# Attention beside a feed-forward network on one core: in the second half of the tokens, two exponentials and the gates share one stay of ScalarE's table

## The chip, the core and the metric

One NeuronCore of a Trainium2 chip runs the whole kernel. The metric is the device time of one launch in microseconds (us), taken as the median of several runs. The core has five engines that work side by side, each through its own queue in order: TensorE (PE; its weight loads are PEld), VectorE (DVE), ScalarE (ACT), GpSimd (POOL) and SyncE (SP), which here only issues transfers. An engine whose next instruction waits for a semaphore holds up everything behind it in its queue.

## The reference

There are 2048 tokens of 512 channels. Everything is fp32.

```python
g = sigmoid((x * gate_w).sum(-1, keepdims=True))           # one gate for each token
q, k, v = (x @ wqkv), split into 32 heads of 16             # scale = 16 ** -0.5
logits[s, w] = q[s] . k[s - 2 * w] * scale                  # w = 0..7, masked before the start
o[s] = sum_w softmax(logits[s])[w] * v[s - 2 * w]
a = o @ wo
b = (gelu(x @ w_gate) * (x @ w_up)) @ w_down                # 1792 hidden channels
return g * a + (1 - g) * b
```

Attention sees only tokens at an even distance, so even and odd tokens never meet. The kernel does the 1024 even tokens first and the 1024 odd ones after them. It calls the two halves parities (`par` 0 and 1).

## The kernel before

**The feed-forward network.** `ffn(par)` runs over 14 channel blocks `f` of 128 hidden channels. `gate_up` computes a block in seven products (a Strassen-like scheme, L459), each of 6 matmuls in split precision. They accumulate in PSUM banks called `p`, of which there are four in turn: `X_`, `W_`, `Z_` and one for the down products. ScalarE copies partial sums out (`W_ <- X_` L539, `copy` L464) and applies gelu (L554 and L570). VectorE adds (`add`, L469, reads a `p` bank), multiplies gelu by up (L473) and takes the low half of the split (`hl`, L476), which needs ScalarE's high half (`hh`, L475). The last product of a block, `a22` by `t4`, and its gelu L570 are put into the next block (`fourth()`). The down products (L502) read `hh` and `hl`.

**The attention.** Each parity has four units of 128 channels (8 heads), `(par, 0)` to `(par, 3)`. A unit goes through these steps, nearly all on VectorE:

- `scores`: four times a product of shifted keys and queries (L225) and a sum over 16 channels (L228), into the tile `lg`; then the mask (L232).
- `exps`: maximum over the 8 places (L241; recorded in `PEAK`), subtraction (L243; recorded in `LESS`), then the exponential on ScalarE (L245).
- `gates(par)`: sigmoid of the gate's logits: an exponential on ScalarE (`en`, L167), then three small steps on VectorE (L170 to L172) that give `g` and `gc`. Once for each parity.
- `softmax` and `gated`: sum (L257), reciprocal (L259), times the gate (L267), times `lg` (L269).
- `mix`: four times values by weights (L287), three sums (L291, L293, L295), and transposes to DRAM (L300, L302).

ScalarE holds one table of functions at a time. Gelu and exp are in different ones, so between a gelu and an exp stands an ACT_TABLE_LOAD. In the first parity the exponentials of units 0 and 1 and the gates already stand together (L245 twice, then L167).

**The order.** `attention()` is a generator that writes these steps in small portions; `pull(budget)` in the feed-forward code takes portions by a price in microseconds. A scheduler then sets each engine's order from priorities, dependencies and its own timeline. `ordered` adds a fixed order on one engine, `after` a wait across engines, and `paced` ties a step to the last matmul.

**The slots.** The tile `kq` holds in its first part the keys of a unit `(par, 0)` and later the values of a unit, in its last part the queries. In `load_kq` the last load of unit (1, 2), its queries, waits for `PEAK`, and in `mix` the value loads of unit (1, 0) do:

```python
for ins in load_slots(v, VS[par, hh][c]):
    if par and not u:
        after(ins, PEAK[-1])
```

These loads (L201, L209, L210) go through SP's queue with the feed-forward's weight loads (`g<-ws` L412, `raw` L438 and L440, `r` L392).

Of the kernel before, what the change touches and what calls it, by code (L numbers as in the profile page):

```python
# [12 lines left out]
AF = mybir.ActivationFunctionType  # L13
# [35 lines left out]
def tile_gated_mix(ctx: ExitStack, tc: tile.TileContext, xt, wqkv, wff, wo, out):  # L49
    nc = tc.nc  # L50
# [69 lines left out]
    z = pool.tile([P, 2, NP], F32, name="z")  # L120
# [42 lines left out]
        if not hh:  # L163
            nc.scalar.activation(z[:, par, jj:jj + 1], ps[:, CU:CU + 1], AF.Copy)

    def gates(par, ex=None):
        first = nc.scalar.activation(en, z[:, par], AF.Exp, scale=-1.0)  # L167
        if ex:
            ordered(first, ex)
        nc.vector.tensor_scalar_add(en, en, 1.0)  # L170
        nc.vector.reciprocal(g[:, par], en)
        nc.vector.tensor_scalar(gc[:, par], g[:, par], -1.0, 1.0, op0=OP.mult, op1=OP.add)  # L172
# [19 lines left out]
    def load_kq(par, u):  # L192
        hh, c = divmod(u, 2)
        k, q = slots_of(u > 0), KQ["a"][:, 2 * NP - 1:]
        if u == 1:
            q = pool.tile([P, 2, BT * UC], F32, name="tb").rearrange("p a (b c) -> p (a b) c", c=UC)
        LG[par, u] = k, q
        if not u:
            return
        loads = load_slots(k, KS[par, hh][c])  # L200
        loads.append(nc.sync.dma_start(q, QS[par, hh][c].rearrange("(p j) d -> p j d", j=NP)))  # L201
        if not par and u < NU - 1:
            for ins in loads:
                after(ins, SCORED[-1])
        elif (par, u) == (1, 2):
            after(loads[-1], PEAK[-1])
# [13 lines left out]
    def scores(par, u):  # L220
        k, q = LG[par, u]
        lg = pool.tile([P, UH, NP, W], F32, name="lg", bufs=2)
        for jj in range(0, NP, 2):
            prod = pool.tile([P, 2, W, UC], F32, name="prod")
            paced(nc.vector.tensor_tensor(prod, spans(k, jj), q[:, jj:jj + 2, None, :].to_broadcast([P, 2, W, UC]),  # L225
                                          op=OP.mult))
            yield 2.3
            nc.vector.tensor_reduce(two_of(lg, jj), prod.rearrange("p j w (h d) -> p (j w) h d", d=DH), axis=AX.X,  # L228
                                    op=OP.add)
            yield 2.3  # L230
        first = lg[:1, :, :NP - 1, :W - 1]
        SCORED[:] = [nc.vector.tensor_tensor(  # L232
            first, first, mask[:1, None, :NP - 1, :W - 1].to_broadcast([1, UH, NP - 1, W - 1]), op=OP.min)]
        LG[par, u] = lg

    def exps(par, *us):

        for u in us:
            lg = LG[par, u]
            m = pool.tile([P, UH, NP], F32, name="m")  # L240
            PEAK[:] = [nc.vector.tensor_reduce(m, lg, axis=AX.X, op=OP.max)]  # L241
            yield 0.7
            LESS[:] = [nc.vector.tensor_tensor(lg, lg, m[:, :, :, None].to_broadcast([P, UH, NP, W]), op=OP.subtract)]  # L243
            yield 0.7
        ex = [nc.scalar.activation(LG[par, u], LG[par, u], AF.Exp, scale=DH ** -0.5) for u in us]  # L245
        if len(us) > 1:
            after(ex[0], LESS[-1])
            ordered(ex[1], ex[0])
            ordered(ex[0], COPIED[-1])
            gates(par, ex[1])  # L250

    def softmax(par, u):
        if par or u != 1:
            yield from exps(par, u) if par or u else exps(par, u, u + 1)
        lg = LG[par, u]
        m = pool.tile([P, UH, NP], F32, name="m")
        nc.vector.tensor_reduce(m, lg, axis=AX.X, op=OP.add)  # L257
        yield 0.7
        nc.vector.reciprocal(m, m)  # L259
        LG[par, u] = lg, m  # L260

    def gated(par, u):
        lg, m = LG[par, u]
        LG[par, u] = lg
        if par and not u:
            gates(par)
        nc.vector.tensor_tensor(m, m, g[:, par, None, :].to_broadcast([P, UH, NP]), op=OP.mult)  # L267
        yield 0.4
        nc.vector.tensor_tensor(lg, lg, m[:, :, :, None].to_broadcast([P, UH, NP, W]), op=OP.mult)  # L269
        yield 0.7  # L270

    def mix(par, u, pause):
        lg = LG.pop((par, u))
        hh, c = divmod(u, 2)
        v = slots_of(u == NU - 1)
# [3 lines that stand above are left out]
            elif (par, u) == (0, NU - 1):  # L279
                after(ins, LESS[-1])  # L280
        yield pause
        tb = pool.tile([P, 2, BT * UC], F32, name="tb")
        for jj in range(0, NP, 2):
            if jj % BT == 0:
                o = pool.tile([P, 4, BT, 32], F32, name="o")
            prod = pool.tile([P, 2, W, UC], F32, name="prod")
            paced(nc.vector.tensor_tensor(prod.rearrange("p j w (h d) -> p (j w) h d", d=DH),  # L287
                                          spans(v, jj).rearrange("p j w (h d) -> p j w h d", d=DH),
                                          two_of(lg, jj)[:, :, :, None].to_broadcast([P, 2 * W, UH, DH]), op=OP.mult))
            yield 2.3  # L290
            nc.vector.tensor_tensor(prod[:, :, :4], prod[:, :, :4], prod[:, :, 4:], op=OP.add)  # L291
            yield 1.2
            nc.vector.tensor_tensor(prod[:, :, :2], prod[:, :, :2], prod[:, :, 2:4], op=OP.add)  # L293
            two = [prod[:, :, i].rearrange("p j (b c) -> p b j c", b=4) for i in range(2)]
            nc.vector.tensor_tensor(o[:, :, jj % BT:jj % BT + 2], *two, op=OP.add)  # L295
            yield 1.1

            if jj % BT == BT - 2:
                t = tb[:, jj // BT]
                nc.vector.transpose(t, o.rearrange("p b t c -> p (b t c)"))  # L300
                for a in range(4):
                    nc.sync.dma_start(OS[par, u, jj // BT][:, :, a].rearrange("b i c -> i b c"),  # L302
                                      t[32 * a:32 * a + 32].rearrange("p (b c) -> p b c", b=4))
                yield 0.7
# [3 lines left out]
    def after(ins, other, cls=mybir.DependencyClass.Sync):  # L308

        tc.add_manual_dep(ins.ins, other.ins.name, mybir.DependencyInfo(cls, mybir.DependencyReason.SCHED_ONLY),  # L310
                          reason="pace")
# [4 lines left out]
    def ordered(ins, other):  # L316
        after(ins, other, mybir.DependencyClass.NoSync)

    def need(*key):
        while key not in done:  # L320
            yield None

    def attention():
        units = [(0, u) for u in range(NU)] + [(1, u) for u in range(NU)]
        yield from need(0, 0)
        load_kq(0, 0)
        yield from scores(0, 0)
        load_kq(0, 1)
        yield from scores(0, 1)
        yield from need(0, 1)  # L330
        scored, mixed = 2, False
        for i, un in enumerate(units):
            if scored == i:
                yield from need(un[0], un[1] // 2 * 2)
                load_kq(*un)
                if un[1]:
                    yield LOAD
                else:
                    load_kq(un[0], 1)
                yield from scores(*un)  # L340
                scored += 1
                mixed = False
            yield from softmax(*un)
            if un == (1, 0):
                yield from scores(*units[scored])
                scored += 1
                yield from need(un[0], 1)
            yield from gated(*un)


            to = units[scored] if scored < len(units) else None
            ahead = to and (to[0], to[1] // 2 * 2) in done
            if ahead:
                load_kq(*to)
            yield from mix(*un, LOAD if mixed else 0.0)
            done.add((*un, "o"))
            mixed = not ahead
            if ahead:
                yield from scores(*to)
                scored += 1  # L360

    fill = attention()
    credit = [0.0]

# [114 lines left out]
    late, COPIED = [], []  # L479
# [740 lines left out]
    en = pool.tile([P, NP], F32, name="en")  # L1220
# [51 lines left out]
```

## Time and profile before

| | |
|---|---|
| median of 3 runs | 597.06 us (596.82 to 597.29) |
| the profiled execution's own time | 596.87 us |
| its span, first to last instruction | 594.8 us |
| busy: PE, DVE, ACT, POOL | 590.1, 529.4, 389.9, 89.2 us |
| granted clock of TensorE | 0.999 |
| ACT_TABLE_LOADs | 18 of 1283 ns: 7 before an exponential of logits (L245), 1 before the gates' (L167), 7 before L570, 2 before L554, 1 at the start (L787) |

All times inside the trace are from the span's start. A row of a timeline has the start, the duration, the engine, the line, the operation, output <- input, the shape and the count, and in brackets how long the engine stood idle before it and what ended that. Successive instructions of one engine overlap slightly at their ends, so the distance between starts is what one costs in a row of work. The second parity's feed-forward runs from about 315 us to the end. The work that the change touches lies between 345 and 460 us.

### The profile page before, as it was taken

Reading aid. Unit: us, or ns where it says so; the run is one execution under the profiler, and the core shown is the slowest. Engines: PE = TensorE matmul, PEld = TensorE weight load, DVE = VectorE, ACT = ScalarE, POOL = GpSimd, SP = SyncE. Lnnn points to the kernel's source line nnn. Section 1 sums busy time; section 2 is a strip of 40 time slices with the busy share of each in tenths; the row PEclk is TensorE's granted clock in tenths of the full one; section 3 lists DMA queues with packets and bytes.
Section 4 is the critical chain, followed back from the end, with each engine's and each line's share of the span. In section 5 each row is a group of like instructions: output and inputs, shape, how many; then the busy total and the mean of one; then the engine's idle time right before and its main releaser. Section 6 shows DMA issues by size and latency. Waiting matters only on the chain.

```text
span 594.8 us, 8195 instructions
## 1 busy us (share of the span) xinstructions
PE 590.1 (99%) x2778; PEld 494.1 (83%) x2778; DVE 529.4 (89%) x618; ACT 389.9 (66%) x668; POOL 89.2 (15%) x121
## 2 busy tenths in 40 slices
PE   9999999999999999999999999999999999999997
PEld 6889988888888888888889988888888888888886
DVE  5997979899998999799989888999999989799952
ACT  5845556787679767788773375677668666885532
POOL 0501001111111111102035000111111111101300
PEclk9999999999999999999999999999999999999999
DMA  8789897988989898998589948795967796737924
GB/s 316 264 250 244 238 306 217 261 245 200 273 215 300 225 261 230 240 312 304 192 249 306 276 137 264 168 244 145 272 157 226 183 269 157 220 109 193 143 57 155
DMA packets 80449, 134.18 MB, mean 226 GB/s; under 512 B 8092, under 2 KB 46362, under 8 KB 80152
## 3 DMA queue, kind: packets, MB, share of 16 engines
q1 hardware_dynamic: 62890, 97.67, 49.9%
q0 software_dynamic: 12576, 32.97, 28.4%
q10 hardware_dynamic: 4942, 3.01, 1.6%
q8 instruction: 22, 0.36, 0.3%
q14 instruction: 19, 0.16, 0.1%
HBM read 68.30 MB, written 38.86 MB: 180 GB/s over the span
## 4 chain that ended last, share of the span: by engine, by line
PE 99%; DVE 0%; ACT 0%; issue 0%
PE p L459 45%; PE acc L502 13%; PE p L502 13%; PE acc L130 8%; PE acc L787 8%; PE p L720 5%; PE p L787 5%; PE acc L720 2%; PE p L79 1%; DVE r L766 0%; ACT rt L768 0%; DVE zero L73 0%
## 5 line engine op out<-in xcount | busy, mean ns | idle before, releaser
L459 PE MATMUL p<-S,g 128*128 128x512 f32 x672 | 166.5, 389 | 0.0
L459 PEld LDWEIGHTS p<-S,g 128*128 128x128 f32 x672 | 125.7, 188 | 25.8
L459 PE MATMUL p<-A,g 128*128 128x512 f32 x504 | 126.7, 390 | 0.0
L459 PEld LDWEIGHTS p<-A,g 128*128 128x128 f32 x504 | 94.3, 188 | 19.6
L417 POOL DMA_DIRECT2D g<-raw x40 | 34.5, 862 | 280.3 <-ACT g L416 208.8
L228 DVE TENSOR_REDUCE lg<-prod 128x128 f32<-128x2048 f32 x32 | 72.9, 2279 | 0.1
L502 PE MATMUL p<-d,hh 128*128 128x512 f32 x224 | 68.5, 389 | 0.0
L502 PE MATMUL acc<-d,hh 128*128 128x512 f32 x224 | 58.1, 389 | 0.0
L287 DVE TENSOR_TENSOR prod<-kq,lg 128x2048 f32<-128x2048 f32 x24 | 54.7, 2279 | 0.9 <-PE p L459 0.5
L421 ACT ACTIVATE g<-raw 128x1024 fp32r<-128x1024 f32 (+1 forms) x40 | 39.5, 991 | 19.0 <-PE p L459 19.0
L502 PEld LDWEIGHTS acc<-d,hh 128*128 128x128 f32 x224 | 42.0, 188 | 8.7
L502 PEld LDWEIGHTS p<-d,hh 128*128 128x128 f32 x224 | 42.0, 188 | 8.7
L416 ACT ACTIVATE g<-raw 128x1024 fp32r<-128x1024 f32 (+1 forms) x40 | 39.5, 987 | 12.0 <-DVE raw L398 4.6
L469 DVE TENSOR_TENSOR c<-p,s 128x512 f32<-128x512 f32 x56 | 37.8, 682 | 6.8 <-PE p L459 6.0
L464 ACT ACTIVATE s<-p 128x512 f32<-128x512 f32 x56 | 33.2, 594 | 15.0 <-PE p L459 13.5
L476 DVE TENSOR_TENSOR hl<-c,hh 128x512 fp32r<-128x512 f32 x56 | 38.1, 680 | 5.5 <-ACT hh L475 5.5
L502 PE MATMUL p<-d,hl 128*128 128x512 f32 x112 | 42.8, 389 | 0.0
L475 ACT ACTIVATE hh<-c 128x512 fp32r<-128x512 f32 x56 | 35.1, 628 | 10.7 <-DVE c L473 10.6
L473 DVE TENSOR_TENSOR c<-c 128x512 f32<-128x512 f32 x56 | 38.2, 682 | 4.3 <-ACT c L570 4.1
L518 ACT ACTIVATE rt<-p 128x512 f32<-128x512 f32 x48 | 28.2, 595 | 20.1 <-PE p L502 20.1
L291 DVE TENSOR_TENSOR prod<-prod 128x1024 f32<-128x1024 f32 x32 | 39.0, 1218 | 0.2
L130 PE MATMUL acc<-d,A 128*128 128x256 f32 (+1 forms) x288 | 37.9, 281 | 0.0
(183 smaller groups left out, 982.0 us busy)
## 6 DMA issues: line engine op xcount, KB each, us to landing
g<-raw POOLq DMA_DIRECT2D x27, 512.0 KB, 6.6
raw<-wff SPq DMA_DIRECT2D x42, 256.0 KB, 3.7
ws<-g SPq DMA_DIRECT2D x14, 768.0 KB, 6.2
g<-ws SPq DMA_DIRECT2D x14, 768.0 KB, 5.4
r<-wff SPq DMA_DIRECT2D x28, 256.0 KB, 4.8
d<-r POOLq DMA_DIRECT2D x24, 256.0 KB, 6.4
g<-raw POOLq DMA_DIRECT2D x13, 384.0 KB, 6.4
os<-tb SPq DMA_DIRECT2D x64, 64.0 KB, 3.8
```

The costliest lines, as they stand in the source:

```text
L130: LAST[:] = [nc.tensor.matmul(ps[:, :cn], a[:, t], w[:, c0:c0 + cn], start=(kc == 0 and n == 0), stop=(kc == KC - 1 and n == 2))]
L228: nc.vector.tensor_reduce(two_of(lg, jj), prod.rearrange("p j w (h d) -> p (j w) h d", d=DH), axis=AX.X, op=OP.add)
L287: paced(nc.vector.tensor_tensor(prod.rearrange("p j w (h d) -> p (j w) h d", d=DH), spans(v, jj).rearrange("p j w (h d) -> p j w h d", d=D ...
L291: nc.vector.tensor_tensor(prod[:, :, :4], prod[:, :, :4], prod[:, :, 4:], op=OP.add)
L416: nc.scalar.activation(lo, raw, AF.Copy, scale=-1.0)
L421: ins = nc.scalar.activation(hi, raw, AF.Copy)
L459: LAST[:] = [nc.tensor.matmul(ps, w_, a_, start=(start and kc == 0 and n == 0), stop=(kc == 1 and n == 2), skip_group_check=True)]
L473: nc.vector.tensor_tensor(ge, ge, up, op=OP.mult)
L476: nc.vector.tensor_tensor(hl_, ge, hh_.bitcast(F32), op=OP.subtract)
L502: ins = nc.tensor.matmul(pp, a[:, ts], w, start=(i == 0 and n == 0 and gr == 0), stop=(i == 1 and n == 2), skip_group_check=True)
L720: ins = nc.tensor.matmul(pa, a, b, start=(first and n == 0), stop=(last and n == 2), skip_group_check=True)
L787: return lambda *args, **kw: self.add(getattr(self.eng, name)(*args, **kw))
```

## The change

Three things move, all in parity 1. The exponentials of units (1, 0) and (1, 1) are issued together by one call of `exps`, with `gates(1)` behind them. For that, the scores of (1, 1) are written ahead of the softmax of (1, 0) instead of behind it. And the tie of the first exponential to the last PSUM copy (`COPIED`) holds for parity 0 alone, as `exps` with two units now runs in parity 1 too.

```diff
-    def gates(par, ex=None):
-        first = nc.scalar.activation(en, z[:, par], AF.Exp, scale=-1.0)
-        if ex:
-            ordered(first, ex)
+    def gates(par, ex):
+        ordered(nc.scalar.activation(en, z[:, par], AF.Exp, scale=-1.0), ex)
...
             ordered(ex[1], ex[0])
-            ordered(ex[0], COPIED[-1])
+            if not par:
+                ordered(ex[0], COPIED[-1])
             gates(par, ex[1])
...
     def softmax(par, u):
-        if par or u != 1:
-            yield from exps(par, u) if par or u else exps(par, u, u + 1)
+        if u != 1:
+            yield from exps(par, u) if u else exps(par, u, u + 1)
...
         LG[par, u] = lg
-        if par and not u:
-            gates(par)
...
-            yield from softmax(*un)
             if un == (1, 0):
                 yield from scores(*units[scored])
                 scored += 1
                 yield from need(un[0], 1)
+            yield from softmax(*un)
             yield from gated(*un)
```

Lines below the edits get smaller numbers: L245 becomes L243, L241 becomes L239, L257 becomes L256, L287 becomes L284, and from L340 on each is smaller by 3 (L539 becomes L536, L570 L567, L469 L466, L473 L470, L502 L499). The text uses the numbers of before.

**ScalarE, where the gates and the first exponential stand.** Before, the gates (`en`) come while the last value projections are still copied out (`c`), with a load of the exp table and, two instructions on, one of the gelu table:

```order
L167 ACT_TABLE_LOAD
L167 ACTIVATE en_580<-z_113 128x8
L160 ACTIVATE c_3578<-acc3_3565 128x256
L464 ACTIVATE s_3589<-p_3582 128x512
L570 ACT_TABLE_LOAD
L570 ACTIVATE c_3597<-p_3213 128x512
```

The exponential of unit (1, 0), whose logits are `lg_3360`, comes one block later, again between two loads. Now both loads at the gates are gone, that exponential has moved two blocks on, and there stand, between the copy `W_ <- X_` (`p_3936`) of block 4 and the gelu of block 3 (`c_3965`), both units' logits (`lg_3360` and `lg_3622`) and the gates:

```order
L536 ACTIVATE p_3936<-p_3929 128x512
L243 ACT_TABLE_LOAD
L243 ACTIVATE lg_3360<-lg_3360 128x512
L243 ACTIVATE lg_3622<-lg_3622 128x512
L167 ACTIVATE en_580<-z_113 128x8
L567 ACT_TABLE_LOAD
L567 ACTIVATE c_3965<-p_3786 128x512
L413 ACTIVATE g1_3980<-raw_3783 128x1024
L461 ACTIVATE s_3954<-p_3947 128x512
```

The copy of `Z_` (`s_3954`) now stands behind that gelu. In the whole program 18 table loads become 14: the pair at the gates and the pair around the exponential of unit (1, 1) are gone, and one later load stands at L554 instead of L570.

**VectorE, behind that stay.** Before, in the same block 4, the adds that free the banks `Z_` (`p_3945`) and `X_` (`p_3925`) stand among the first quarters of `mix` (1, 0):

```order
L295 TENSOR_TENSOR o_3908<-prod_3909 128x4x64
L469 TENSOR_TENSOR c_4004<-p_3945,s_3976 128x512
L257 TENSOR_REDUCE m_4410<-lg_3648 128x64
L287 TENSOR_TENSOR prod_3981<-kq_268,lg_3360 128x2048
L473 TENSOR_TENSOR c_3995<-c_3995,c_4004 128x512
L259 RECIPROCAL m_4410<-m_4410 128x64
L469 TENSOR_TENSOR c_4029<-p_3925,s_3952 128x512
```

Now both units' softmax and gating and the first product of `mix` (1, 0) stand ahead of the first of these adds (`c_4007<-p_3947`). These 12 instructions begin with `c_3965`, which needs the gelu behind the stay; the add of `X_` (`c_4028`) follows three further on:

```order
L470 TENSOR_TENSOR c_3965<-c_3965,c_3887 128x512
L264 TENSOR_TENSOR m_3901<-m_3901,g_114 128x64
L170 TENSOR_SCALAR gc_579<-g_114 128x8
L266 TENSOR_TENSOR lg_3360<-lg_3360,m_3901 128x512
L256 TENSOR_REDUCE m_4410<-lg_3622 128x64
L258 RECIPROCAL m_4410<-m_4410 128x64
L284 TENSOR_TENSOR prod_3922<-kq_268,lg_3360 128x2048
L473 TENSOR_TENSOR hl_3969<-c_3965,hh_3968 128x512
L264 TENSOR_TENSOR m_4410<-m_4410,g_114 128x64
L288 TENSOR_TENSOR prod_3922<-prod_3922 128x2x512
L266 TENSOR_TENSOR lg_3622<-lg_3622,m_4410 128x512
L466 TENSOR_TENSOR c_4007<-p_3947,s_3978 128x512
```

On PE the products of block 4 are the same 66 matmuls from its first product to the first product of block 5, with `a22` by `t4` of block 3 moved one product earlier and some down products moved.

**SP, the loads for `kq`.** Before, the queries of unit (1, 2) (`qs11`) and the values of unit (1, 0) (`vs10`) stand on both sides of a weight load:

```order
L440 DMA raw_3666<-wff 128x2x256
L201 DMA kq_268<-qs11_104 128x1024
L412 DMA g0_3801<-ws40_1335 128x1536
L209 DMA kq_268<-vs10_100 128x896
L210 DMA kq_268<-vs10_100 128x1024
```

Now they stand ten places further on, behind weight loads of the following blocks and the keys of unit (1, 2), and in one piece. `PEAK` is now the maximum of unit (1, 1), since one call of `exps` takes both:

```order
L207 DMA v_862<-ks11_102 128x896
L208 DMA v_862<-ks11_102 128x1024
L435 DMA raw_3926<-ws61_1466 128x512
L437 DMA raw_3926<-wff 128x2x256
L389 DMA r_3924<-wff 128x512
L199 DMA kq_268<-qs11_104 128x1024
L207 DMA kq_268<-vs10_100 128x896
L208 DMA kq_268<-vs10_100 128x1024
L409 DMA g0_4067<-ws60_1605 128x1536
```

## The prediction

> **What bounds the kernel now.** I read the page's first part and its chain first, then the busy time by stretches, then the timelines of the engines around the edit.
>
> ```profile
> PE 590.1 (99%) x2778; PEld 494.1 (83%) x2778; DVE 529.4 (89%) x618; ACT 389.9 (66%) x668; POOL 89.2 (15%) x121
> ...
> PE 99%; DVE 0%; ACT 0%; issue 0%
> ```
>
> TensorE is busy for 590.1 of 594.8 us, and the chain that ended last is TensorE from end to end. In the stretches (columns: length, then busy time of PE, PEld, DVE, ACT, POOL, then clock, transfer share, GB/s) the two that the edit rearranges, and the tail:
>
> ```profile
> 380.00:400.00 20.00, 20.00 (x90) 16.55 (x89) 19.50 (x20) 13.64 (x23) 2.95 (x4) 1.00 0.93 234
> 400.00:420.00 20.00, 20.00 (x90) 16.55 (x89) 19.79 (x25) 14.07 (x22) 1.70 (x2) 1.00 0.68 178
> ...
> 570.00:595.00 25.00, 21.25 (x94) 17.27 (x92) 7.47 (x12) 4.55 (x8) 0.00 (x0) 0.97 0.31 106
> ```
>
> TensorE never pauses there, and the granted clock is 1.00. Only 594.8 - 590.1 = 4.7 us of the span are without a matmul, and 25.00 - 21.25 = 3.75 us of these are the last output copies and stores. So work taken off ScalarE or VectorE gives nothing back by itself: the change takes no matmul away, and there is no pause in the middle to close. It can only open one. The question is whether some bank or operand now comes later than TensorE asks for it.
>
> **The change part by part.** The table loads first (timeline of ScalarE):
>
> ```profile
> 346.86 1.28 ACT L167 ACT_TABLE_LOAD   x1
> 348.16 0.21 ACT L167 ACTIVATE en<-z 128x8 f32<-128x8 f32 x1
> ...
> 349.82 1.28 ACT L570 ACT_TABLE_LOAD   x1
> ...
> 367.65 1.28 ACT L245 ACT_TABLE_LOAD   x1
> 368.94 0.64 ACT L245 ACTIVATE lg<-lg 128x512 f32<-128x512 f32 x1
> 369.48 0.62 ACT L475 ACTIVATE hh<-c 128x512 fp32r<-128x512 f32 x1
> ...
> 375.80 0.61 ACT L539 ACTIVATE p<-p 128x512 f32<-128x512 f32 x1
> 376.43 1.28 ACT L570 ACT_TABLE_LOAD   x1
> 377.72 0.60 ACT L570 ACTIVATE c<-p 128x512 f32<-128x512 f32 x1
> ...
> 390.01 0.58 ACT L539 ACTIVATE p<-p 128x512 f32<-128x512 f32 x1 [0.76 <-PE p L459]
> ```
>
> Four of 18 loads go, 4 x 1.28 = 5.1 us of ScalarE. Worth on the span: nothing, since ScalarE is busy 66% of it and TensorE did not wait.
>
> Two waits of VectorE go as well (timeline of VectorE, idle time before the row in brackets):
>
> ```profile
> 348.40 0.17 DVE L170 TENSOR_SCALAR en<-en 128x8 f32<-128x8 f32 x1 [2.44 <-ACT en L167]
> ...
> 362.22 0.67 DVE L241 TENSOR_REDUCE m<-lg 128x64 f32<-128x512 f32 x1
> ...
> 369.61 0.69 DVE L257 TENSOR_REDUCE m<-lg 128x64 f32<-128x512 f32 x1 [2.69 <-ACT lg L245]
> ```
>
> That is 2.44 + 2.69 = 5.1 us. They don't turn into a shorter span either; until 390 us they only let VectorE run ahead of TensorE, and it then waits for the gelu outputs of blocks that TensorE has not finished.
>
> The cost is in block 4, where the stay now stands. I walk the queues from TensorE's fixed marks (timeline of TensorE; the last product of block 3 ahead of its add, the first products of blocks 4 and 5, and `a22` by `t4` of block 4):
>
> ```profile
> 385.73 1.52 PE L459 MATMUL p<-S,g 128*128 128x512 f32 x6
> ...
> 388.45 1.52 PE L459 MATMUL p<-A,g 128*128 128x512 f32 x6
> ...
> 403.41 1.52 PE L459 MATMUL p<-A,g 128*128 128x512 f32 x6
> ...
> 406.59 1.52 PE L459 MATMUL p<-A,g 128*128 128x512 f32 x6
> ```
>
> From 388.45 to 403.41 are 66 matmuls, 0.2267 us each, in both kernels.
>
> ScalarE: the copy L539 starts at 390.01. By the distances of the rows above, the load follows 0.63 later (375.80 to 376.43), at 390.64; the first exponential 1.29 later, at 391.93; the second 0.54 later (368.94 to 369.48) and the gates' another 0.54 later, at 393.01; the gelu's load 0.21 later, at 393.22; the gelu 1.29 later, from 394.51 to 395.11.
>
> Do the exponentials have to wait for VectorE? The add of block 3 that reads the product of 385.73 can start when that ends, 385.73 + 1.52 = 387.25. Behind it stand one multiply, the maximum L241 and the subtraction L243, 0.6 us each: the subtraction is done at about 389.7, 2.2 us before 391.93. So no.
>
> VectorE: its multiply L473 of that gelu starts about 0.03 behind it (348.16 + 0.21 to 348.40), at 395.15. In front of the adds that free the banks stand the instructions that the order shows. Their prices are distances between starts in this piece of before:
>
> ```profile
> 400.15 2.28 DVE L287 TENSOR_TENSOR prod<-kq,lg 128x2048 f32<-128x2048 f32 x1
> 402.35 0.69 DVE L473 TENSOR_TENSOR c<-c 128x512 f32<-128x512 f32 x1
> 402.95 0.55 DVE L259 RECIPROCAL m<-m 128x64 f32<-128x64 f32 x1
> 403.41 0.63 DVE L469 TENSOR_TENSOR c<-p,s 128x512 f32<-128x512 f32 x1
> 403.95 1.22 DVE L291 TENSOR_TENSOR prod<-prod 128x1024 f32<-128x1024 f32 x1
> 405.08 0.22 DVE L267 TENSOR_TENSOR m<-m,g 128x64 f32<-128x64 f32 x1
> 405.22 0.69 DVE L476 TENSOR_TENSOR hl<-c,hh 128x512 fp32r<-128x512 f32 x1
> 405.82 0.69 DVE L293 TENSOR_TENSOR prod<-prod 128x512 f32<-128x512 f32 x1
> 406.42 0.69 DVE L269 TENSOR_TENSOR lg<-lg,m 128x512 f32<-128x512 f32 x1
> ```
>
> L287 takes 2.20, L291 1.13, L259 0.46, L267 0.14, the 512-wide ones 0.60. So: L473 0.60, L267 0.14, L172 about 0.1, L269 0.60, L257 0.60, L259 0.46: the first product of `mix` stands at 395.15 + 2.50 = 397.65. Then L287 2.20, L476 0.60, L267 0.14, L291 1.13, L269 0.60 = 4.67: the add of `Z_` starts at 402.32 and ends 0.69 later, at 403.01. TensorE asks for that bank at 403.41: 0.4 us to spare, where before there were more than four:
>
> ```profile
> 398.48 0.67 DVE L469 TENSOR_TENSOR c<-p,s 128x512 f32<-128x512 f32 x1
> ```
>
> The add of `X_` stands three steps of 0.60 later, from 404.12 to 404.81. In the new order TensorE asks for it with `a22` by `t4` right behind the six matmuls of 403.41, at 404.77 (before: at 406.59). That is 0.04 us too late, so I put 0 to 0.3 us here for the small gaps between dependent instructions that the sum leaves out, and take 0.1.
>
> The first product of `mix` also needs the value loads, which now wait for the maximum of unit (1, 1). Before, SP had the three out 0.03 to 1.4 us behind the maximum of unit (1, 0) (timeline of SP, then the DMA issues between 355 and 380 us, then of the whole page; the last number is issue to landing):
>
> ```profile
> 362.92 0.33 SPq L201 DMA_DIRECT2D kq<-qs  x1
> ...
> 364.25 0.58 SPq L210 DMA_DIRECT2D kq<-vs  x1
> ```
>
> ```profile
> kq<-vs SPq DMA_DIRECT2D x1, 512.0 KB, 7.1
> ```
>
> ```profile
> kq<-vs SPq DMA_DIRECT2D x6, 512.0 KB, 8.2
> ```
>
> Now the maximum ends at about 389.1 (387.25 + 2 x 0.6, and 0.67 for itself). Without the weight load between them the three go out 0.42 apart (1.33 us for three steps before), the last at 390.0. It lands at 390.0 + 7.1 = 397.1, or by the page's median at 398.2, against the 397.65 at which VectorE gets there. I take 397.1, from the row of this very load: no wait, but 0.55 us from one.
>
> Behind that, VectorE lags. From 404.72, the end of the step of the add of `X_`, to the second transposes of `mix` (1, 0) stand three more rounds of L287, L291 and L293 (3.93 each), eight steps of 0.60 and four of about 0.4: 404.72 + 11.8 + 4.8 + 1.6 = 422.9, against 420.67 before, 2.2 us later. The banks and halves that TensorE asks for up to 465 us keep more than 1 us in that walk, and the orders agree again at the end. The lag is absorbed at the latest where VectorE idled before:
>
> ```profile
> 420.67 0.70 DVE L300 STREAM_TRANSPOSE tb<-o 128x512 f32<-128x512 f32 x1
> ...
> 485.98 0.69 DVE L476 TENSOR_TENSOR hl<-c,hh 128x512 fp32r<-128x512 f32 x1 [1.81 <-ACT hh L475]
> ```
>
> The sum: -5.1 us of loads and -5.1 us of waits, worth 0, and +0.1 us of pause at 404.8. On the profiled execution, 596.87 us with 594.8 of span, that makes 597.0; against the median, 597.06, which lies 0.2 higher, 597.2. A measurement of this kernel can tell about 0.2%, 1.2 us, from no change, so this is no change.
>
> **A rule against it.** ScalarE's loads are followed here at once: L539 ends at 376.41 and the load starts at 376.43, the load ends at 377.71 and the gelu starts at 377.72. The Trainium skill's page "ScalarE: Activation LUTs", section "What ACT_TABLE_LOAD costs", has 1283 ns for a load, as here, but adds a drain of about 1380 ns for each switch of set. By that page the gelu of the stay would come 2 x 1.38 = 2.76 us later than I put it.
>
> **The rivals.**
>
> *The values land late (slower, 0.13).* For it: 0.55 us of margin on a path of SP, queues and memory, and a page median that is already 0.55 us too late. Against: the one earlier pair landed in 7.1 us. Every 0.1 us past 397.65 is 0.1 us of pause at `X_`. It decides from 1.2 us late on (landing after 398.85, 8.9 us from issue); a landing in 10 to 13 us, at 400 to 403, gives 2.4 to 5.4 us: 599.6 to 602.6.
>
> *VectorE's lag opens a pause later (slower, 0.07).* If the lag of 2.2 us meets a bank that TensorE wants without any margin left, up to 2.2 us are lost there; it decides from 1.2 us on: 598.4 to 599.4. Against it: nowhere in before does TensorE wait, though VectorE is busy 19.8 of 20 us in the stretch to 420.
>
> *ScalarE is parked in the stay (slower, 0.04).* If VectorE's subtraction comes after 391.93 instead of at 389.7, gelu, copies and adds all move by the excess. It decides from 2.2 + 1.2 = 3.4 us of error in my walk; 5 us of error gives 2.8 us: 600.0.
>
> *A switch costs more than its load (slower, 0.02).* With a gap of 1.4 us at both switches, the rows shown would have to be the exception: both adds come 2.76 us later, and the pause at `X_` grows to about 2.8 us, 600.0. That is the case of the page's rule; the rows above speak against it.
>
> *It comes out faster (0.02).* It would need a shorter tail or fewer matmul cycles; 3.75 us at the end is all there is, and its order is unchanged. More than 0.3 us, 596.7, I can't find.
>
> **How the numbers follow.** Forecast: a pause of 0 to 1.1 us, chance 0.72, 597.2 us. Slower: 0.13 + 0.07 + 0.04 + 0.02 = 0.26. Faster by over 0.2%: 0.02. The range starts at 596.7, below the fastest of the runs by the noise of before, and goes to 599.4, which holds the forecast, the lag's rival and the small end of the late values: 0.72 and about 0.10 of the 0.26.
>
> **What would show it.** Right: no pause of TensorE longer than 0.3 us between 315 and 590 us; 14 table loads; no wait of VectorE at L170; L257 waiting some 2 to 3 us once, until about 392.6; the gelu at about 394.5. Wrong: a wait of VectorE's first `mix` product for `kq<-vs` around 397 us, then a pause of TensorE before the product at 403.41 or the one behind it; or ScalarE waiting for VectorE ahead of the first exponential; or a busy time of TensorE that is not 590.1 us.

## The result

The changed kernel takes 600.34 us (median of 9 runs, 599.37 to 601.45) beside 597.06 us before. The ratio is 1.005, with a 95% interval of 1.0041 to 1.006: it is slower by 0.5%, 3 us. Measured again later beside other runs of before, the ratio was 1.0042 (1.0028 to 1.0056). The profiled execution took 600.01 us with a span of 598.2 us, 3.4 us more than before.

In this part lines have the numbers of the changed kernel: L536 is the copy `W_ <- X_`, L567 the gelu of `a22` by `t4`, L466 the adds, L473 the low half `hl`, L284 the first step of `mix`, L515 the copy `rt <- p` of a down product, L499 the down products. The experiments' kernels have a few lines more, so that their numbers differ by some units. The builder is the scheduler that sets each engine's order, and a mark of TensorE is the start of a matmul that stands at the same place in both runs.

### The profile page after: what moved, and what is told of

It is laid out like the page before. It is cut to its first block, busy times and chain, and to the rows that moved or that the text cites. A ratio compares the mean times of both kernels' runs of the same rounds, so it can differ in the third digit from the quotient of the medians.

```text
span 598.2 us, 8193 instructions
## 1 busy us (share of the span) xinstructions
PE 590.8 (99%) x2778; PEld 493.5 (83%) x2778; DVE 531.4 (89%) x618; ACT 384.2 (64%) x664; POOL 89.2 (15%) x121
## 4 chain that ended last, share of the span: by engine, by line
PE 95%; DMA 2%; DVE 1%; issue 0%; ACT 0%; SPq 0%; DVEq 0%; ACTq 0%
PE p L456 43%; PE acc L499 12%; PE p L499 12%; PE acc L130 8%; PE acc L784 7%; PE p L717 5%; PE p L784 5%; PE acc L717 2%; DMA kq<-vs 1%; DMA raw<-xt 1%; DVE prod L284 0%; DVE c L466 0%; ACT g L413 0%; DVE c L470 0%; DVE lg L266 0%
## 5 line engine op out<-in xcount | busy, mean ns | idle before, releaser
L499 PE MATMUL p<-d,hh 128*128 128x512 f32 x224 | 68.4, 390 | 0.0
L499 PE MATMUL acc<-d,hh 128*128 128x512 f32 x224 | 58.6, 390 | 0.0
L284 DVE TENSOR_TENSOR prod<-kq,lg 128x2048 f32<-128x2048 f32 x24 | 54.7, 2278 | 0.9 <-PE p L456 0.5
L499 PEld LDWEIGHTS acc<-d,hh 128*128 128x128 f32 x224 | 42.0, 188 | 9.1 <-DMA d<-r 0.3
L499 PEld LDWEIGHTS p<-d,hh 128*128 128x128 f32 x224 | 42.0, 188 | 9.0 <-ACT p L493 0.3
L470 DVE TENSOR_TENSOR c<-c 128x512 f32<-128x512 f32 x56 | 38.3, 684 | 8.1 <-ACT c L567 7.8
L466 DVE TENSOR_TENSOR c<-p,s 128x512 f32<-128x512 f32 x56 | 37.9, 684 | 6.5 <-PE p L456 5.5
L473 DVE TENSOR_TENSOR hl<-c,hh 128x512 fp32r<-128x512 f32 x56 | 38.0, 681 | 5.0 <-ACT hh L472 5.0
L499 PE MATMUL p<-d,hl 128*128 128x512 f32 x112 | 42.4, 389 | 0.0
L515 ACT ACTIVATE rt<-p 128x512 f32<-128x512 f32 x48 | 27.8, 590 | 15.3 <-PE p L499 14.9
```

The lines of the kernel that those rows point to most:

```text
L470: nc.vector.tensor_tensor(ge, ge, up, op=OP.mult)
L473: nc.vector.tensor_tensor(hl_, ge, hh_.bitcast(F32), op=OP.subtract)
L499: ins = nc.tensor.matmul(pp, a[:, ts], w, start=(i == 0 and n == 0 and gr == 0), stop=(i == 1 and n == 2), skip_group_check=True)
```

## The profile after

The busy time and the chain (page of the changed kernel, its first and fourth part):

```profile
PE 590.8 (99%) x2778; PEld 493.5 (83%) x2778; DVE 531.4 (89%) x618; ACT 384.2 (64%) x664; POOL 89.2 (15%) x121
...
PE 95%; DMA 2%; DVE 1%; issue 0%; ACT 0%; SPq 0%; DVEq 0%; ACTq 0%
```

TensorE does the same 2778 matmuls in nearly the same busy time. What is new lies between them: the chain now leaves TensorE for 5% of the span. The stretches (columns as in the prediction) say where:

```profile
380.00:400.00 20.00, 20.00 (x90) 16.56 (x89) 16.22 (x22) 15.00 (x25) 2.55 (x3) 1.00 0.95 269
400.00:420.00 20.00, 19.79 (x86) 15.75 (x86) 19.86 (x25) 12.55 (x20) 1.70 (x2) 1.00 0.78 185
420.00:440.00 20.00, 18.33 (x82) 14.86 (x81) 19.54 (x18) 10.84 (x18) 2.57 (x3) 1.00 0.82 213
440.00:460.00 20.00, 20.00 (x90) 16.56 (x89) 18.54 (x21) 13.75 (x23) 1.77 (x3) 1.00 0.81 226
```

A full stretch has 90 matmuls (x90). The second has 86 and the third 82: 4 and 8 matmuls of 0.227 us are missing, 0.9 and 1.8 us, at a clock of 1.00. There are two pauses here.

**The stay itself** went as forecast (timeline of ScalarE). TensorE is 0.7 us later here than before, so 0.7 is to be added to the forecast's times:

```profile
390.78 0.58 ACT L536 ACTIVATE p<-p 128x512 f32<-128x512 f32 x1 [0.30 <-PE p L456]
391.38 1.28 ACT L243 ACT_TABLE_LOAD   x1
392.68 1.16 ACT L243 ACTIVATE lg<-lg 128x512 f32<-128x512 f32 x2
393.74 0.19 ACT L167 ACTIVATE en<-z 128x8 f32<-128x8 f32 x1
393.94 1.28 ACT L567 ACT_TABLE_LOAD   x1
395.24 0.60 ACT L567 ACTIVATE c<-p 128x512 f32<-128x512 f32 x1
```

**The first pause.** TensorE (timeline), the last down products ahead of block 5 and the twelve matmuls of its `X_` and of `a22` by `t4`:

```profile
403.67 0.61 PE L499 MATMUL p<-d,hl 128*128 128x512 f32 x2
404.35 3.44 PE L456 MATMUL p<-A,g 128*128 128x512 f32 x12
```

Two matmuls are 0.45 us, so the twelve are 404.35 - 404.12 = 0.23 us late, and they take 3.44 us where an undisturbed row of twelve takes 2.88 (below, at 434.38). Together that is 0.8 us. What they wait for are VectorE's adds (timeline of VectorE):

```profile
395.87 0.69 DVE L470 TENSOR_TENSOR c<-c 128x512 f32<-128x512 f32 x1 [1.20 <-ACT c L567]
...
396.73 0.69 DVE L266 TENSOR_TENSOR lg<-lg,m 128x512 f32<-128x512 f32 x1
397.46 0.69 DVE L256 TENSOR_REDUCE m<-lg 128x64 f32<-128x512 f32 x1
398.18 0.55 DVE L258 RECIPROCAL m<-m 128x64 f32<-128x64 f32 x1
398.93 2.29 DVE L284 TENSOR_TENSOR prod<-kq,lg 128x2048 f32<-128x2048 f32 x1 [0.19 <-DMA kq<-vs]
...
403.61 0.68 DVE L466 TENSOR_TENSOR c<-p,s 128x512 f32<-128x512 f32 x1
...
405.41 0.68 DVE L466 TENSOR_TENSOR c<-p,s 128x512 f32<-128x512 f32 x1
```

L284 starts 3.06 us behind L470, not 2.50: 0.37 us are longer steps, mainly the two around the second unit's sum L256 (0.73 and 0.72 us, where the forecast took 0.60), and 0.19 us are a wait for the values. The add of `Z_` ends at 404.29, when TensorE is already waiting, and the add of `X_`, which the second six of the twelve need, at 406.09.

**The values** came late on SP (timeline, and SP's waits between 386 and 394 us: total, times, longest):

```profile
391.32 0.33 SPq L389 DMA_DIRECT2D r<-wff  x1
391.82 0.33 SPq L199 DMA_DIRECT2D kq<-qs  x1
392.24 0.38 SPq L207 DMA_DIRECT2D kq<-vs  x1
392.67 0.42 SPq L208 DMA_DIRECT2D kq<-vs  x1
```

```profile
SPq L389 <- DMA d<-r: 2.7, 1, 2.7
```

The weight load `r<-wff` in front of them waited 2.7 us for the transfer that still read its buffer.

**The second pause** is the larger one (timeline of TensorE, then of ScalarE, then one row of VectorE):

```profile
434.38 2.88 PE L456 MATMUL p<-A,g 128*128 128x512 f32 x12
437.10 0.61 PE L499 MATMUL p<-d,hl 128*128 128x512 f32 x2
439.38 2.79 PE L456 MATMUL p<-S,g 128*128 128x512 f32 x11 [1.67 <-ACT rt L515]
```

```profile
437.30 0.60 ACT L567 ACTIVATE c<-p 128x512 f32<-128x512 f32 x1 [4.24 <-PE p L456]
437.79 1.05 ACT L413 ACTIVATE g<-raw 128x1024 fp32r<-128x1024 f32 x1
438.74 1.07 ACT L515 ACTIVATE rt<-p 128x512 f32<-128x512 f32 x2
```

```profile
433.95 0.68 DVE L473 TENSOR_TENSOR hl<-c,hh 128x512 fp32r<-128x512 f32 x1
```

The product at 439.38 is `Z_` of block 7. It needs the bank of a down product that L515 must copy out first. That down product gets its last matmul, with the low half `hl`, only at 437.10, and two matmuls later TensorE has nothing else to do: 439.38 - 437.55 = 1.83 us, and a small gap of 0.11 follows. Yet that low half was there at 434.63. Before, the last low half came in front of the twelve matmuls (first row, TensorE), the last of the two copies was done at 434.19 (second row, ScalarE), and the product `Z_` started at 437.87 without a wait:

```profile
433.11 0.39 PE L502 MATMUL p<-d,hl 128*128 128x512 f32 x1
...
433.59 0.60 ACT L518 ACTIVATE rt<-p 128x512 f32<-128x512 f32 x1 [0.53 <-PE p L502]
```

The order of TensorE's queue shows what changed. Before, the bank of the second down product is `p_4288` (the first one's low half stands just above these rows):

```
L502 MATMUL p_4288<-d_4083,hh_4222 128x512 x2
L502 MATMUL p_4288<-d_4083,hl_4223 128x512
L459 MATMUL p_4303<-A_2570,g0_4192 128x512 x3
L459 MATMUL p_4303<-A_2571,g0_4192 128x512 x3
L459 MATMUL p_4183<-A_2574,g1_4107 128x512 x3
L459 MATMUL p_4183<-A_2575,g1_4107 128x512 x3
L502 MATMUL acc0_3680<-d_4210,hh_4283 128x512 x2
```

After, with `p_4267` and `p_4290`:

```
L499 MATMUL p_4290<-d_4085,hh_4226 128x512 x2
L456 MATMUL p_4306<-A_2570,g0_4196 128x512 x3
L456 MATMUL p_4306<-A_2571,g0_4196 128x512 x3
L456 MATMUL p_4187<-A_2574,g1_4109 128x512 x3
L456 MATMUL p_4187<-A_2575,g1_4109 128x512 x3
L499 MATMUL p_4267<-d_4085,hl_4227 128x512
L499 MATMUL p_4290<-d_4085,hl_4227 128x512
L456 MATMUL p_4324<-S_2724,g0_4196 128x512 x3
```

The two low-half matmuls moved behind twelve others and stand right in front of the product that needs their bank, and the eight `acc` matmuls that stood between are gone from there. So 0.8 + 1.9 = 2.7 us of the 3.4 are found.

**The other 0.7 us** lie ahead of block 4, in three parts of some 0.2 us each. Two of them differ from run to run. At the start, the first product of the first block stands at 44.41 us before, at 44.65 here, and between 44.16 and 46.03 in the runs below, while TensorE's order is the same up to there. At 268 us a transfer of the next tokens (`raw<-xt`) lands late, which some of the runs below don't have. The third belongs to the change: at 378 us TensorE waits 0.3 us for the transfer `d<-r`, which took 5.0 us from issue to landing, where it took 3.4 before. Every run below in which the value loads are late has this wait, with 5.0 to 5.1 us for that transfer; before, x3 and x7 have neither (3.4 to 3.8 us). In these three SP issues its next weight loads (`raw`) 1.4 to 2.5 us behind `d<-r`, in all the others 0.2 us ahead of it. That the loads side by side are the reason fits, but no run tested it alone.

## The experiments

All kernels but one are the changed kernel with one or two edits. The pauses are those of each profiled run, summed from the distances between matmul starts, without the 0.2 us at 378; the ratio is to the runs of before on the same chip.

| run | pause at 404, us | pause at 437, us | median, us | ratio (95%) |
|---|---|---|---|---|
| changed kernel | 0.8 | 1.9 | 600.34 | 1.005 (1.0041 to 1.006) |
| the same, again | 0.5 | 1.9 | 599.90 | 1.0042 (1.0028 to 1.0056) |
| x1, copies ahead of the gelu | 1.4 | 1.9 | 599.79 | 1.0047 (1.0035 to 1.0059) |
| x2, weight copy behind the copies | 0.4 | 1.5 | 599.40 | 1.0046 (1.0031 to 1.0061) |
| x3, loads early | 0 | 0 | 596.65 | 0.9994 (0.9982 to 1.0006) |
| x4, second softmax late | 0.4 | 0 | 597.93 | 1.002 (1.0006 to 1.0034) |
| x5, low halves first | 1.4 | 0 | 597.83 | 1.0022 (1.0007 to 1.0037) |
| x6, gates back | 0.5 | 1.9 | 599.38 | 1.0044 (1.0032 to 1.0056) |
| x7, scores ahead alone | 0 | 0 | 596.87 | 1.0003 (0.9994 to 1.0012) |
| x8, weight load behind the values | 0.4 | 1.9 | 599.27 | 1.0036 (1.0023 to 1.0049) |
| x9, x5 and x8 | 0.5 | 0 | 597.94 | 1.0012 (1.0003 to 1.002) |
| x10, x4 and x8 | 0 | 0 | 597.17 | 1.0001 (0.9993 to 1.001) |

### x1 and x2: is it ScalarE's queue?

x1 ties the gelu of block 6 behind the two copies; x2 ties only the weight copy behind them.

```diff
-            nc.scalar.activation(RT[BT + t], pp, AF.Copy)
+            KEPT[:] = [nc.scalar.activation(RT[BT + t], pp, AF.Copy)]
...
+            if (par, f) == (1, 6):        # x1
+                ordered(gelu, rts)        # rts: the last copy of block 6
...
+        if (par, f, i) == (1, 8, 1):      # x2
+            ordered(neg, KEPT[-1])        # neg: the weight copy L413
```

> Theory A (the 1.83 us pause at 437 us in the changed kernel is ScalarE's queue order alone: the gelu of block 6 and the 128x1024 weight copy stand in front of the two copies rt<-p that free the bank of TensorE's next product). This kernel is the changed one with one tie: the gelu of block 6 after the two copies. A expects the pause at 437 us gone, the pause of about 0.75 us at 404 us left as it is, and 600.3 - 1.8 = 598.5 us. Rival B (the pause comes from VectorE being some 2 us behind after block 4, and shows wherever a bank is next due) expects a pause of similar size to come up again elsewhere between 425 and 465 us and the time to stay at 600 +- 0.4 us.

> Half a dose of the first: only the 128x1024 weight copy of block 8 is tied behind the two copies rt<-p; the gelu stays ahead of them. Theory A expects the pause at 437 us shorter by the 0.95 us that this copy holds the queue: 0.9 us in place of 1.83, and 600.3 - 0.95 = 599.4 us. Rival B expects no change of the time beyond 0.3 us.

ScalarE and TensorE in x1 (timelines):

```profile
437.66 1.06 ACT L413 ACTIVATE g<-raw 128x1024 fp32r<-128x1024 f32 x1 [4.24 <-PE p L456]
438.63 1.06 ACT L515 ACTIVATE rt<-p 128x512 f32<-128x512 f32 x2
```

```profile
437.46 0.61 PE L499 MATMUL p<-d,hl 128*128 128x512 f32 x2
439.75 1.65 PE L456 MATMUL p<-S,g 128*128 128x512 f32 x6 [1.67 <-ACT rt L515]
```

The gelu is behind the copies and the pause is the same to 0.01 us. The weight copy, too, waits for TensorE's last product, and it still holds the queue. In x2:

```profile
437.15 1.08 ACT L517 ACTIVATE rt<-p 128x512 f32<-128x512 f32 x2
438.11 1.07 ACT L413 ACTIVATE g<-raw 128x1024 fp32r<-128x1024 f32 x1
```

```profile
437.80 1.66 PE L458 MATMUL p<-S,g 128*128 128x512 f32 x6 [0.72 <-ACT rt L517]
439.72 1.64 PE L458 MATMUL p<-S,g 128*128 128x512 f32 x6 [0.26 <-ACT p L538]
```

The pause shrinks by 0.95 us as theory A said, but the copy `W_ <- X_` now stands behind the weight copy and half of the gain is lost again at 439.72. So theory A fell: ScalarE's queue sets only a part of the length. In x1 no pause came up elsewhere, as rival B expected, though its 599.79 us lies in B's range. That x2's median is the 599.4 us of theory A is luck: its pause at 437 us is 1.5 us and not 0.9, and the one at 404 us is shorter than was taken. In both runs the copies could not start before TensorE had done the matmuls at 437, and this is what led to x5.

### x5: the place of two matmuls

```diff
+        down_last = LAST[-1] if (par, f) == (1, 6) else None
...
-            product(X_, "a22", w["t4"], False)
+            product(X_, "a22", w["t4"], False, down_last)   # its matmuls: ordered(..., down_last)
```

> Theory A is put right: in the first two runs ScalarE's two copies could not start earlier, since TensorE's last two matmuls into their banks (the low halves of block 6, p<-d,hl) stand behind the first product of block 7 and a22 by t4 of block 6, in the order that is built when VectorE is late with that low half. A2: the price at 437 us is the place of these two matmuls on TensorE. This kernel is the changed one with one tie: a22 by t4 of block 6 after them. A2 expects no pause at 437 us, the 0.75 us at 404 us unchanged, and 600.3 - 1.9 = 598.4 us. Rival B (VectorE's lag of some 2 us has to be paid at some bank) expects TensorE to wait for VectorE's low half ahead of these two matmuls by 0.3 us or more, or for another bank up to 465 us, and 599.5 us or more.

TensorE and ScalarE in x5 (timelines):

```profile
405.77 3.46 PE L456 MATMUL p<-A,g 128*128 128x512 f32 x12 [0.69 <-DVE c L468]
...
437.18 0.61 PE L501 MATMUL p<-d,hl 128*128 128x512 f32 x2
437.63 1.52 PE L456 MATMUL p<-A,g 128*128 128x512 f32 x6
438.99 2.20 PE L456 MATMUL p<-S,g 128*128 128x512 f32 x9
```

```profile
437.60 1.09 ACT L517 ACTIVATE rt<-p 128x512 f32<-128x512 f32 x2 [3.11 <-PE p L501]
```

The second pause is gone: the six matmuls behind the low halves cover the copy. TensorE waits neither for the low half nor elsewhere up to 465 us, so rival B (the lag has to be paid at some bank) is refuted for this place. The first pause is longer in this profiled run, 1.4 us: VectorE waited 0.8 us for the values there, where it waited 0.19 us in the changed kernel. The median, 597.83 us, is 0.6 us under the 598.4 expected. The tie also let the builder set later rows anew, so x5 is not a change of two rows alone.

### x8: the queue that held the values

```diff
-        nc.sync.dma_start(RD[f], wff[f, :, 1024:])
+        ins = nc.sync.dma_start(RD[f], wff[f, :, 1024:])
+        if f == 5 and VALS:
+            ordered(ins, VALS[-1])        # VALS: the value loads of mix (1, 0)
```

> The changed kernel with one row of SP's queue moved and all other queues the same: the weight load r<-wff, which waited 2.7 us for the transfer that reads its buffer and held the value loads behind it, is tied behind the value loads. If the held queue is what made the values late, they go out by about 391.0 and VectorE's first mix product starts at about 398.7 without a wait, 0.2 us earlier than in the changed kernel; the pause at 404 us shrinks from 0.75 to about 0.55 us and no more, since VectorE's own queue (the second unit's sum and reciprocal stand ahead of it) sets the rest: 600.1 us. If late values were the whole of that pause, it would go: 599.6 us.

SP and VectorE in x8 (timelines):

```profile
390.15 0.43 SPq L208 DMA_DIRECT2D kq<-vs  x1
390.69 0.37 SPq L390 DMA_DIRECT2D r<-wff  x1
```

```profile
398.04 2.23 DVE L285 TENSOR_TENSOR prod<-kq,lg 128x2048 f32<-128x2048 f32 x1
```

The values go out 2.5 us earlier than in the changed kernel (1.9 us by TensorE's marks, as this run is 0.6 us ahead there), and no wait for them is left. The first pause goes to 0.4 us (0.55 was expected), the second stays. The median, 599.27 us, is 0.8 us under the expected 600.1; beside the runs of before on its chip the ratio is 1.0036, and the intervals of this run and of the changed kernel overlap, so the time alone shows nothing here. The pauses do: late values are not the whole of the first. The changed kernel measured again shows the same from the other side: no wait for the values, and still 0.5 us. In the profiled runs in which the product waited 0.8 to 0.9 us for them (x1, x5), the first pause is 1.4 us.

### x4 and x10: VectorE's own queue

x4 puts the second unit's sum, reciprocal and gating behind the first `mix`; x10 adds x8's edit.

```diff
+        if (par, u) == (1, 1):
+            ordered(total, MIXED[-1])     # total: the sum L256; MIXED: the last sum of mix (1, 0)
```

> The changed kernel with the sum, reciprocal and gating of unit (1, 1) tied behind the last quarter of mix (1, 0), so that they don't stand ahead of the adds of block 4; the value loads stay late. Theory A expects the first mix product still at about 398.9, now waiting for the value loads by 1.3 us, the adds of block 4 about 0.75 us earlier and the pause at 404 us gone; and since the order at block 7 comes out with the copies ahead of the gelu, no pause at 437 either: 597.2 to 597.6 us. A rival D (the late values are what costs) expects the 0.75 us to stay: 597.8 us or more.

> The changed kernel with the second unit's sum, reciprocal and gating behind the first mix, and the weight load behind the value loads; the common maximum stays. If the 0.4 us that is left at 404 us is VectorE's own queue (two instructions of the second unit, 1.3 us, ahead of the first mix product, two more behind it), it goes only as far as the values are there: they land at about 397 us, so that the first product starts at about 397.5 and both adds are in time: no pause of TensorE between 315 and 590 us and 596.9 us. If something else holds block 4 back, 0.3 us or more stay there.

VectorE's first step of `mix` in x4, then that step and the two adds in x10 (timelines):

```profile
402.76 2.29 DVE L286 TENSOR_TENSOR prod<-kq,lg 128x2048 f32<-128x2048 f32 x1 [1.55 <-DMA kq<-vs]
```

```profile
397.17 2.29 DVE L288 TENSOR_TENSOR prod<-kq,lg 128x2048 f32<-128x2048 f32 x1 [0.27 <-DMA kq<-vs]
...
401.12 0.68 DVE L472 TENSOR_TENSOR c<-p,s 128x512 f32<-128x512 f32 x1
...
403.25 0.68 DVE L472 TENSOR_TENSOR c<-p,s 128x512 f32<-128x512 f32 x1
```

With VectorE's queue mended alone, the wait for the values takes the place of the two instructions (1.55 us, at 402.76 in a run that is 3.8 us behind the changed kernel's by waits for transfers ahead of 95 us), and 0.4 us of pause stay, neither the 0 that theory A expected nor the 0.75 of rival D. The median, 597.93 us, lies in rival D's range, but its runs reach from 596.98 to 601.53. With both mended, the adds are some 2.0 and 1.6 us earlier than in the changed kernel (this run is 0.5 us ahead there), and the pause is gone. So the first pause has two causes, each about long enough by itself: the values land late, and two instructions of the second unit, 1.3 us, stand in front of the product (two more, 0.7 us, stand between it and the adds). In both kernels the built order also has the low halves ahead of the twelve products, and there is no second pause. The ratio of x10 is 1.0001, with the common maximum and the 14 table loads kept.

### x9: the two ties together

> The low-halves tie and the weight-load tie of the last two runs together, with the common maximum, the 14 table loads and the second unit's softmax still ahead of the first mix product. If the two causes add, the pause at 437 us is gone, the one at 404 us is about 0.4 us as with the weight-load tie alone, and the time is 0.4 to 0.5 us above before: 597.3 us. If the values' landing were not what makes the runs of the low-halves tie scatter up to 601.8 us, the scatter stays.

The second pause is gone and 0.5 us of the first stay; 1.0012 is 0.7 us of 597. The median is 0.6 us above the expected 597.3, in part by transfers of the next tokens that land late at 268 us (0.6 us in its profiled run). Its runs reach from 597.3 to 598.9 us, those of x5 from 597.2 to 601.8. The scatter is smaller, as expected, but the two were run on different chips and none of the long runs has a profile, so that the values' landing is the reason is not shown.

### x3: one line that undoes it all

Only `PEAK` is changed: the loads wait for the maximum of unit (1, 0) again. Exponentials, gates and the scores stay as changed.

```diff
-            PEAK[:] = [nc.vector.tensor_reduce(m, lg, axis=AX.X, op=OP.max)]
+            top = nc.vector.tensor_reduce(m, lg, axis=AX.X, op=OP.max)
+            if not (par and u == 1):
+                PEAK[:] = [top]
```

> The changed kernel with the value loads of the first mix and the query load of unit (1, 2) tied to the maximum of unit (1, 0) again, as before the change; table loads stay at 14. The order that is built from it has the two copies ahead of the gelu in block 7 by itself, and the first product of mix ahead of the second unit's sum and reciprocal. Theory A expects both pauses gone, 597.2 us, and VectorE's first product at about 397.5 without a wait for a transfer. A rival C (the long stay of ScalarE's table itself is what costs: three exponentials and two loads in a row in front of the gelu) expects the 0.75 us at 404 us to stay: 597.8 us or more.

The chain on its page, and VectorE's first step of `mix` and the two adds (timeline):

```profile
PE 99%; DMA 1%; ACT 0%; DVE 0%; issue 0%
```

```profile
396.56 2.29 DVE L286 TENSOR_TENSOR prod<-kq,lg 128x2048 f32<-128x2048 f32 x1
...
401.56 0.63 DVE L468 TENSOR_TENSOR c<-p,s 128x512 f32<-128x512 f32 x1
...
404.38 0.68 DVE L468 TENSOR_TENSOR c<-p,s 128x512 f32<-128x512 f32 x1
```

The whole loss is back. With the loads early, the built order puts the product ahead of the second unit's two instructions, and the low halves in their old place. The stay with its three exponentials is unchanged, so rival C is refuted.

### x6 and x7: the other parts alone

x6 puts the gates back behind the softmax. x7 is the kernel before with the scores of (1, 1) written ahead, and nothing else.

> The changed kernel with the gates of parity 1 behind the softmax of unit (1, 0) again instead of in the stay; the order built from it puts them back to block 1, with two more table loads (16), and leaves TensorE's and SP's queues as in the changed kernel. If joining the gates and the two loads is worth nothing or costs nothing, both pauses stay and the time is 600.3 +- 0.4 us. If the third exponential in the stay is what makes block 4 late, the gelu comes 0.2 us earlier, and the pause at 404 us shrinks by 0.2 us at most.

> The kernel before with only one part of the change: the scores of (1, 1) are written ahead of the softmax of (1, 0); exponentials and gates stay apart, with 18 table loads. If the cost comes from the common maximum that the value loads wait for (theory A), this is 597.0 +- 0.3 us. If writing the scores ahead is itself what pushes VectorE behind (rival B), pauses of TensorE show between 400 and 465 us, and the time is 598 us or more.

Two table loads more (16) and the gates back in block 1 leave both pauses, with TensorE's order unchanged: joining the gates is worth nothing that can be seen. The median, 599.38 us, misses the expected 600.3 +- 0.4; the ratio, 1.0044, lies between the two of the changed kernel. Writing the scores ahead costs nothing either: 1.0003, no pause, with 18 loads; its value loads still go out at 364 us (SP's timeline), since each unit has its own maximum there:

```profile
364.41 0.57 SPq L210 DMA_DIRECT2D kq<-vs  x1
```

### The changed kernel again

> The changed kernel as it is, on the chip and beside the runs of before that the two other kernels of this call have: 599.4 to 600.4 us, with the pause of 1.83 us at 437 us and 0.5 to 1.3 us at 404 us, the latter by when the values land.

## Why the prediction was wrong, step by step

- **No gain is possible; loads and VectorE's waits are worth 0.** Right. 14 loads, ScalarE 5.7 us less busy, no wait at the gates' first step on VectorE (L170 before, L168 here), one wait of 2.1 us at L256. x3 has all of that and measures 0.9994; x7 has all 18 loads and measures 1.0003.
- **The walk through ScalarE's stay.** Right to 0.05 us: with the 0.7 us, the first exponential was forecast at 392.63 (392.68) and the gelu at 395.21 (395.24). The Trainium skill's page "ScalarE: Activation LUTs", section "What ACT_TABLE_LOAD costs", agrees with the trace in the 1283 ns of a load; the drain of about 1380 ns that it adds is not seen: the gelu starts 0.02 us behind the load, and the first exponential too.
- **"It lands at 390.0 + 7.1 = 397.1."** Wrong in the issue. The walk started the three loads at the maximum and left out the weight load `r<-wff` that stood in front of them in SP's order, and its own wait of 2.7 us. With the 0.7 us, the last was forecast to go out at 390.7 and to land at 397.8. It went out at 392.67 and landed at 398.8: 6.1 us of flight, shorter than the 7.1 taken, made up for half, and that was luck (other runs have up to 7.9).
- **"That is 0.04 us too late ... 0 to 0.3 us ... take 0.1."** The mechanism and the place were right, the size was not: 0.8 and 0.5 us in two profiled runs. The six steps ahead of the first product took 2.87 us, not 2.50, and the values could add their own wait. So the add of `Z_`, forecast 0.4 us in time, was late too.
- **"The banks and halves that TensorE asks for up to 465 us keep more than 1 us in that walk."** This is the step that failed: the sum has 0 for everything behind the add of `X_`, and 1.9 of the 3.4 us were lost there. The lag of VectorE came as walked and somewhat larger (the second transposes of `mix` (1, 0) start at 424.83, 4.2 us later than before, of which 1.5 are TensorE's own delay). But the walk went along VectorE's queue with TensorE's order as it was before. The new order was given, and in it two low-half matmuls stood directly in front of the product that needs their bank. A walk of TensorE's queue with ScalarE's copy behind it could have found the pause from rows of before: a copy of 0.6 us with a gelu and a weight copy in front. That the order came with the later loads, x3 shows: with the loads tied to the earlier maximum again, the low halves are back in their place.
- **The rivals.** "The lag opens a pause later" had the right size for that pause (up to 2.2 us) by coincidence, for no bank behind block 4 was late by VectorE's lag on the chip: the low half lay ready 2.5 us before it was used, and x5 removed the pause without making VectorE faster. "The values land late" came in as the lesser part, 0 to 0.9 us of waiting. Parked ScalarE and the dearer switch did not happen.

What stays open is why the builder moved the low halves. In the kernels here in which VectorE has less in front of the adds of block 4 (x3, x4, x10), it left them in their old place by itself, which fits a builder that expected the low half late; its own reckoning was not seen.

## What to carry to other kernels

A variable that pacing hangs on (here `PEAK`) is part of what a refactoring changes: merging two calls made loads wait for the later of two maxima, and this, with the orders that the builder made from it, cost all of the 3 us while the table loads that the change saved were worth nothing. When the busiest engine is at 99%, walk its own new order, bank by bank, and not only the queue of the engine that gets late: two matmuls moved in a fixed order cost 1.9 us here, the lateness of VectorE itself 0.5 to 0.8 us. And a load that gets a later condition also gets the waits of whatever now stands in front of it in its queue.

## What the runs showed that I had not expected

- The same transfer, 512 KB of values, took between 6.1 us from issue to landing (changed kernel) and 7.9 us (x5) in the same place of the program. In x1, where it went out as long behind TensorE's marks as in the changed kernel, 6.8 us instead of 6.1 went with a first pause of 1.4 us instead of 0.8.
- The start, with TensorE's order the same, scatters by up to 1.9 us between runs (44.16 to 46.03 us for the first product of block 0). A pause of 0.5 us can't be told from a median alone here; the distances of matmul starts show it.
- Mending one queue can change nothing at all: x1 moved the gelu out of the way, and the pause kept its length to 0.01 us, because the next instruction in that queue waited for the same event.
